# Seven block products for two row tiles in the second MLP product, other engines for some copies, and no filler products in the first batch

## The chip, the cores and the metric

The kernel runs on one core of a Trainium2 chip. The core has a matrix engine (TensorE, "PE" in the profile; its weight loads are "PEld"), three engines for elementwise work (VectorE "DVE", ScalarE "ACT", GpSimd "POOL"), SyncE ("SP"), which here only issues transfers, and 16 DMA engines. They run side by side and wait for each other by semaphores. SBUF is the working memory, PSUM holds what TensorE writes. The metric is the device time of one execution in microseconds.

## What is computed

First an attention over chunks of keys: for each query, the six best of 24 chunks of 32 keys are chosen by an upper bound on their scores, and only these (and only earlier keys) take part in the softmax. Then a layer norm and a two-layer MLP with a residual.

```python
q, k, v: (4, 8, 768, 64)                      # batch, heads, sequence, head dim
ub   = sum(max(q * k_min, q * k_max), -1)     # per chunk of 32 keys
sel  = chunk is among the top 6 of ub         # and causal
attn = softmax(where(sel & causal, q @ k.T / 8, -1e9))
x    = (attn @ v) as (4, 768, 512)
xn   = (x - mean) / sqrt(var + 1e-6) * g_ln
out  = x + relu(xn @ w_ch1) @ w_ch2           # w_ch1: 512 x 2048, w_ch2: 2048 x 512
```

## The kernel before

The work is cut into 16 pairs of heads (four to a batch; pair g belongs to batch g // 4) and, for the MLP, into eight halves (batch b, half r) of three row tiles of 128 rows each. Every piece of work is a small function, and one long string, `ORDER`, lists all calls: `smm.5.0.0` calls `smm(5, 0, 0)`, and a suffix such as `@1` sets `other[0]`, which a function may use to choose another engine. The loop at the end calls them in that order and makes every engine keep the order of its own instructions. So each engine is a queue in program order: an instruction that waits holds back all that stands behind it on its engine.

For a pair g of batches 1 to 3 (g from 4 on) the stages are:

- `ldb` loads q and k; `turn` transposes them on VectorE; `qhi`, `qlo`, `qrel` make q in two f16 parts and their positive parts; `kbound`, `kdiag` make the chunk bounds of k.
- `bounds` (L320) forms the upper bounds on TensorE, `select` chooses chunks on VectorE (L346 to L352), `maskt` and `mring` bring the mask into place.
- Operands of the scores lie in rings of four buffers, `QA`, `QB` (queries and mask rows) and `KA`, `KB` (keys). `kcopy` fills the keys on ScalarE. `qring` brings the queries into QA and QB by two transfers on SyncE's queue (L267, L268).
- `smm` (L414) makes scores into PSUM tiles `mm` (two buffers), `sexp` (L422) takes the exponential on ScalarE, `diag` (L429) masks the diagonal on GpSimd, `values` (L445) multiplies with v, `norm` (L459, L460) divides on VectorE and `pstat` takes statistics.

For a half (b, r) of the MLP: `centre` (L484, L487) makes xc = (x - mean) * g as f16 on VectorE, `rstd` (L495, L498) the reciprocal deviation, with the power on GpSimd; `xt` (L504) transposes xc by DMA; `m1` (L513) is the first product, two blocks of 128 hidden columns a call; `relu` (L525, or L523 on VectorE) writes `hT`; `m2` (L538) is the second product: a row tile has one PSUM bank `yp` and 16 products of 512 columns, four a call; `fin` (L547) adds x and stores the tile. The scale 1/deviation is applied there, after the second product:

```python
nc.vector.scalar_tensor_tensor(
    ot[:, cs], h["yp", i][:, cs], h["rstd"][:, i:i + 1], xh(b, r)[:, i].rearrange("p h d -> p (h d)")[:, cs],
    op0=ALU.mult, op1=ALU.add,
)
```

`busy(o)` (L117) multiplies constants into a part of a PSUM tile that nobody reads; `turn`, `bounds`, `smm` and others call it in batch 0, in a number that the suffix sets (none without a suffix). `w1` and `w2` load the weights in four chunks each from GpSimd's queue; chunk j of w2 holds the four blocks that `m2.b.r.i.j` uses. In PSUM the pool `ps_t` has four single banks, shared by `tr`, `ub`, `trh`, `sm` and `yp`.

Of the kernel before, what the change touches and what calls it, by code (L numbers as in the profile page):

```python
# [10 lines left out]
ALU = mybir.AluOpType  # L11
# [8 lines left out]
def kernel(  # L20
# [239 lines left out]
    def qrel(g):  # L260
        qh, ql, rh, rl = (st[g][nm][:, P:] for nm in ("qh", "ql", "rh", "rl"))
        nc.vector.tensor_scalar_max(rh, qh, 0.0)
        nc.vector.scalar_tensor_tensor(rl, qh, 0.0, ql, op0=ALU.is_gt, op1=ALU.mult)

    def qring(g, i=None):
        if i is None:
            nc.sync.dma_start(QA[g % NK][0:64, :], st[g]["qh"][0:64, :])  # L267
            nc.sync.dma_start(QB[g % NK][64:P, :], st[g]["qh"][64:P, :])  # L268
            return
        qt = st[g]["qn", i]  # L270
        a, z = span(g, i)
        nc.scalar.activation(QA[g % NK][0:64, a * P:z * P], qt[0:64, :], ACTF.Copy, scale=QS)
        nc.scalar.activation(QB[g % NK][64:P, a * P:z * P], qt[64:P, :], ACTF.Copy, scale=QS)
# [64 lines left out]
    def select(g, i=None):  # L338
# [4 lines left out]
        if g >= HP:  # L343
            ubt = smp.tile([P, NT - 1, 2, NCH], F32, name="ubt", tag="ubt", bufs=1)
            ubm = smp.tile([P, NT - 1, 2, NCH], F32, name="ubm", tag="ubm")
            nc.vector.tensor_tensor(ubt, ub[:, :, 1], causf, ALU.add)  # L346
# [131 lines left out]

    def centre(b, r):
# [3 lines left out]
        for i in range(TR):  # L483
            nc.vector.bn_aggr(h["mv"][:, i, :], h["st"][:, i])  # L484
        for i in range(TR):
            xs = xh(b, r)[:, i].rearrange("p h d -> p (h d)")
            nc.vector.scalar_tensor_tensor(  # L487
                h["xc"][:, i, :], xs, h["mv"][:, i, 0:1], gall, op0=ALU.subtract, op1=ALU.mult,
            )
# [37 lines left out]
    def last(b, r, i):  # L527
        return (b, r, i) == (B - 1, NR - 1, TR - 1)

    def m2(b, r, i, j):  # L530
# [3 lines left out]
        n, cs = 4, slice(0, DM)  # L534
        if last(b, r, i):
            n, cs = 8, slice(0, DM - P) if j < 2 else slice(DM - P, DM)
        for kt in range(n * j % KT2, n * j % KT2 + n):
            nc.tensor.matmul(  # L538
                h["yp", i][:, cs], h["hT"][:, kt, i * P:(i + 1) * P], w2b[:, kt, cs],
# [3 lines left out]
    def fin(b, r, i, e=None):  # L543
        h = hf[b, r]
        cs = (slice(0, DM), slice(0, DM - P), slice(DM - P, DM))[0 if e is None else 1 + e]
        ot = outp.tile([P, DM], F32, name="ot", tag="ot")
        nc.vector.scalar_tensor_tensor(  # L547
            ot[:, cs], h["yp", i][:, cs], h["rstd"][:, i:i + 1], xh(b, r)[:, i].rearrange("p h d -> p (h d)")[:, cs],
            op0=ALU.mult, op1=ALU.add,
        )  # L550
        s = TR * r + i
        nc.sync.dma_start(out[b, s * P:(s + 1) * P, cs], ot[:, cs])
# [4 lines left out]
        consts ld.0.0 rrows.0.0 rinit.0 ld.1.0 ld.2.0 warm.8 turn.0.qn.0 rrows.2.1@1 qpos.0.0 rrows.3.1 qring.0.0  # L557
        turn.0.kn.0 rinit.2 kbound.0.0 rinit.1 turn.1.qn.0 kcopy.0.0 ld.3.0 turn.1.kn.0 kbound.1.0 kdiag.0.0
        qring.1.0 rrows.1.0 rinit.3 turn.2.qn.0@3 ld.0.1 rrows.0.1 bounds.0.0@2 kdiag.1.0 rrows.1.1 qpos.1.0
        select.0.0 turn.2.kn.0 kcopy.2.0@1 kcopy.1.0 qpos.2.0 bounds.1.0@2 kbound.2.0 qring.2.0 maskt.0.0 select.1.0  # L560
        kdiag.2.0 turn.3.kn.0 mring.0.0@1 ld.1.1 turn.3.qn.0 kcopy.3.0 rrows.3.0 ldv.2.0 maskt.1.0 qpos.3.0
        kbound.3.0 smm.0.0.0 ldv.0.0 mring.1.0 bounds.2.0@2 select.2.0 turn.0.kn.1 qring.3.0 rrows.2.0 smm.0.0.1
        turn.1.kn.1 turn.0.qn.1 ld.2.1 kdiag.3.0 sexp.0.0.0 ldv.3.0 kcopy.0.1 qpos.0.1 kbound.1.1 sexp.0.0.1
        kbound.0.1 kcopy.1.1 ldv.1.0 kdiag.0.1 smm.1.0.0@2 bounds.3.0@2 maskt.2.0 diag.0.0 qring.0.1 bounds.0.1
        sexp.1.0.0 select.3.0 values.0.0 maskt.3.0 mring.2.0 kdiag.1.1 smm.1.0.1 select.0.1 smm.2.0.0 w1.2.3 w1.1.3
        w1.0.2 norm.0.0 sexp.1.0.1 ldb.4.qn smm.2.0.1 sexp.2.0.0 mring.3.0 maskt.0.1 ld.3.1 turn.1.qn.1 sexp.2.0.1
        qpos.1.1 ldb.5.kn mring.0.1 diag.1.0 values.1.0 norm.1.0 diag.2.0 pstat.0.0 smm.3.0.0 pstat.1.0
        turn.2.kn.1@1 sexp.3.0.0 kbound.2.1 qring.1.1 turn.4.qn smm.3.0.1@2 sexp.3.0.1 bounds.1.1 values.2.0
        smm.0.1.0 diag.3.0 select.1.1 kcopy.2.1 smm.0.1.2@1 values.3.0 sexp.0.1.0 norm.2.0 sexp.0.1.2 norm.3.0
        turn.2.qn.1 smm.0.1.1 pstat.2.0 sexp.0.1.1 kdiag.2.1@1 qpos.2.1 smm.0.1.3 qring.2.1 ldv.0.1 turn.3.kn.1  # L570
        maskt.1.1 pstat.3.0 qhi.4 kcopy.3.1 mring.1.1 diag.0.1 smm.1.1.0@2 ldb.4.kn bounds.2.1 sexp.1.1.0 sexp.0.1.3
        centre.0.0 xt.0.0.0 xt.0.0.1 select.2.1 turn.3.qn.1@3 kbound.3.1 qlo.4 smm.1.1.3 xt.0.0.2 ldb.5.qn qring.4
        maskt.2.1 turn.4.kn sexp.1.1.3 smm.1.1.2 values.0.1 kdiag.3.1 qpos.3.1 qrel.4 kbound.4 sexp.1.1.2 smm.1.1.1
        bounds.3.1 mring.2.1 sexp.1.1.1 w1.3.3 late select.3.1 kdiag.4 diag.1.1 norm.0.1 turn.5.kn m1.0.0.0 kcopy.4
        turn.5.qn relu.0.0.0 kbound.5 m1.0.0.4 ldv.1.1 qring.3.1 ldb.6.kn relu.0.0.4 w2.0.0 m1.0.0.2 relu.0.0.2
        bounds.4 pstat.0.1 m1.0.0.10 qhi.5 m1.0.0.6 relu.0.0.10 relu.0.0.6 maskt.3.1 kcopy.5@1 kdiag.5 m1.0.0.8
        m1.0.0.12 relu.0.0.8 m1.0.0.14 relu.0.0.12 ldb.6.qn smm.2.1.0 select.4 qlo.5 rstd.0.0 qrel.5 relu.0.0.14
        sexp.2.1.0 bounds.5 smm.2.1.1 smm.2.1.2 ldv.2.1 ldv.3.1 w2.1.0 turn.6.kn sexp.2.1.1 values.1.1 smm.2.1.3
        mring.3.1 diag.2.1 sexp.2.1.2 select.5 sexp.2.1.3 norm.1.1 smm.3.1.0 maskt.4 sexp.3.1.0 smm.3.1.2 kbound.6
        mring.4 maskt.5 w2.2.1 w2.3.1 sexp.3.1.2 smm.3.1.1 ldb.7.kn smm.3.1.3 sexp.3.1.1 ldb.7.qn values.2.1 qring.5  # L580
        sexp.3.1.3 mring.5 pstat.1.1 norm.2.1 smm.4.1.0 diag.3.1 sexp.4.1.0 smm.4.0.0 kdiag.6 values.3.1 m2.0.0.0.0
        norm.3.1 pstat.2.1 pstat.3.1 smm.5.0.0 kcopy.6 sexp.4.0.0 sexp.5.0.0 m2.0.0.2.0 m2.0.0.1.0 smm.4.0.1
        m2.0.0.0.1 sexp.4.0.1 turn.6.qn qhi.6 centre.0.1 qlo.6 smm.4.1.3 turn.7.kn smm.4.1.2 sexp.4.1.3 sexp.4.1.2
        m2.0.0.1.1 turn.7.qn qrel.6 smm.4.1.1 rstd.0.1 m2.0.0.2.1 kcopy.7 kbound.7 m2.0.0.0.2 m2.0.0.2.2 sexp.4.1.1
        m2.0.0.1.2 smm.5.1.0 xt.0.1.0 bounds.6 m2.0.0.2.3 select.6 xt.0.1.1 xt.0.1.2 ldb.8.kn sexp.5.1.0 qhi.7
        m1.0.1.0 qlo.7 diag.4.0 ldv.4 turn.8.kn qring.6 m1.0.1.6 relu.0.1.0 relu.0.1.6 m2.0.0.0.3 m1.0.1.14 ldb.8.qn
        kdiag.7 fin.0.0.0 qrel.7 fin.0.0.2 relu.0.1.14 ldb.9.qn diag.4.1 m1.0.1.2 kbound.8 maskt.6 ldv.5 relu.0.1.2
        ldv.6 kcopy.8 ldb.10.qn m2.0.0.1.3 qring.7 turn.8.qn mring.6 m1.0.1.4 relu.0.1.4 diag.5.0 m1.0.1.8 qhi.8
        relu.0.1.8 ldv.7 fin.0.0.1 values.4.0 norm.4.0 smm.5.0.1 bounds.7 qlo.8 smm.5.1.1 qrel.8 select.7 sexp.5.0.1
        kdiag.8 sexp.5.1.1 smm.5.1.3 values.4.1 diag.5.1 sexp.5.1.3 smm.5.1.2 ldb.9.kn values.5.0 ldb.10.kn  # L590
        ldb.12.qn sexp.5.1.2 smm.6.1.0 sexp.6.1.0 bounds.8 norm.4.1 smm.6.1.2 norm.5.0 values.5.1 sexp.6.1.2
        smm.6.1.1 sexp.6.1.1 pstat.4.1 m2.0.1.0.0 m1.0.1.10 qring.8 m1.0.1.12 m2.0.1.0.1 relu.0.1.10 relu.0.1.12
        smm.6.0.0 sexp.6.0.0 turn.9.qn maskt.7 select.8 smm.6.0.1 sexp.6.0.1 m2.0.1.0.2 pstat.4.0 maskt.8 smm.6.1.3
        qhi.9@1 diag.6.0 m2.0.1.0.3 mring.7 pstat.5.0 norm.5.1 fin.0.1.0 smm.7.0.0 diag.6.1 sexp.6.1.3 sexp.7.0.0
        smm.7.0.1 values.6.1 diag.7.0 values.6.0 mring.8 sexp.7.0.1 norm.6.1 smm.7.1.0 smm.7.1.2 values.7.0 qlo.9
        m2.0.1.2.0 norm.6.0 norm.7.0 sexp.7.1.0 smm.7.1.3 sexp.7.1.2 m2.0.1.1.0 pstat.6.0 pstat.7.0 smm.7.1.1
        ldb.11.kn sexp.7.1.3 m2.0.1.1.1 sexp.7.1.1 diag.7.1 turn.9.kn centre.1.0 xt.1.0.0 smm.8.1.0 m2.0.1.2.1
        sexp.8.1.0 smm.8.0.0 m2.0.1.2.2 kbound.9 m2.0.1.1.2 smm.8.1.2 m2.0.1.2.3 xt.1.0.2 kcopy.9 qrel.9 sexp.8.0.0
        values.7.1 sexp.8.1.2 smm.8.0.1 pstat.6.1 xt.1.0.1 smm.8.1.3 sexp.8.0.1 norm.7.1 sexp.8.1.3 kdiag.9 diag.8.1
        ldb.11.qn pstat.5.1 m2.0.1.1.3 smm.8.1.1 fin.0.1.2 bounds.9 pstat.7.1 centre.1.1 sexp.8.1.1 xt.1.1.0  # L600
        m1.1.0.0 m1.1.0.2 relu.1.0.0 xt.1.1.1 m1.1.0.4 relu.1.0.2 m1.1.0.6 relu.1.0.4 relu.1.0.6 m1.1.0.8 relu.1.0.8
# [89 lines left out]
```

## Time and profile before

| | |
|---|---|
| time, median of 3 (lowest, highest) | 288.89 us (288.71, 291.12) |
| profiled execution: device time, span of the trace | 290.76 us, 288.7 us |
| TensorE busy | 271.7 us (94%) |
| VectorE, ScalarE, GpSimd busy | 211.8, 180.8, 94.1 us |
| granted TensorE clock, mean | 0.981 |
| read from memory, written | 27.53 MB, 6.29 MB |

The span is the time from the first to the last instruction. The page divides it into 40 slices of 7.2 us, with one digit each for an engine's busy share in tenths. A group line gives a source line, engine, operation and tiles, how often, the busy time and the mean duration in ns, and then the time the engine stood idle just before. The chain of waits is followed back from the last instruction: at each step to what released it.

### The profile page before, as it was taken

Reading aid. Unit: us, or ns where it says so; the run is one execution under the profiler, and the core shown is the slowest. Engines: PE = TensorE matmul, PEld = TensorE weight load, DVE = VectorE, ACT = ScalarE, POOL = GpSimd, SP = SyncE. Lnnn points to the kernel's source line nnn. Section 1 sums busy time; section 2 is a strip of 40 time slices with the busy share of each in tenths; the row PEclk is TensorE's granted clock in tenths of the full one; section 3 lists DMA queues with packets and bytes.
Section 4 is the critical chain, followed back from the end, with each engine's and each line's share of the span. In section 5 each row is a group of like instructions: output and inputs, shape, how many; then the busy total and the mean of one; then the engine's idle time right before and its main releaser. Section 6 shows DMA issues by size and latency. Waiting matters only on the chain.

```text
span 288.7 us, 6793 instructions
## 1 busy us (share of the span) xinstructions
PE 271.7 (94%) x2628; PEld 181.8 (63%) x2628; DVE 211.8 (73%) x629; ACT 180.8 (63%) x241; POOL 94.1 (33%) x165
## 2 busy tenths in 40 slices
PE   5999999992799999999899999999999999999994
PEld 2889997671355777566656776566667745555541
DVE  5699999998079998999699979998797483221212
ACT  3688999694185977865775877667777522513210
POOL 8505615781039203182442643141072200100100
PEclk9999999998599999999999999999999999999999
DMA  6999997999949989489919691927011112310102
GB/s 141 203 179 177 202 156 126 167 151 194 139 84 70 188 162 182 78 116 133 172 29 185 112 148 20 136 81 163 16 43 59 39 20 72 93 39 36 73 0 110
DMA packets 136063, 32.42 MB, mean 112 GB/s; under 512 B 127072, under 2 KB 132960, under 8 KB 136032
## 3 DMA queue, kind: packets, MB, share of 16 engines
q1 hardware_dynamic: 106640, 24.39, 43.7%
q0 software_dynamic: 29248, 7.34, 27.4%
q8 instruction: 20, 0.33, 0.5%
q10 hardware_dynamic: 144, 0.26, 0.4%
q14 instruction: 11, 0.09, 0.1%
HBM read 27.53 MB, written 6.29 MB: 117 GB/s over the span
## 4 chain that ended last, share of the span: by engine, by line
PE 81%; DMA 8%; DVE 7%; ACT 2%; issue 1%; ACTq 0%; DVEq 0%
PE yp L538 27%; PE mm L513 25%; PE mm L414 11%; PE sm L445 6%; DMA QA<-q 3%; PE ub L333 3%; DMA xT<-xc 3%; PE ub L320 2%; ACT pt L422 2%; PE tr L236 2%; DMA raw<-in_k_dram 2%; PE tr L117 2%; DVE xc L487 1%; PE trh L361 1%; PE ub L117 1%; PE mm L117 1%
## 5 line engine op out<-in xcount | busy, mean ns | idle before, releaser
L422 ACT ACTIVATE pt<-mm 128x1024 f16<-128x1024 f32 (+2 forms) x96 | 84.6, 917 | 30.0 <-PE mm L414 28.9
L538 PE MATMUL yp<-w2b,hT 128*128 128x512 f16 (+2 forms) x400 | 94.8, 377 | 0.0
L513 PE MATMUL mm<-xT,w1b 128*128 128x384 f16 x512 | 87.9, 326 | 0.8 <-DMA xT<-xc 0.8
L525 ACT ACTIVATE hT<-mm 128x768 f16<-128x768 f32 x61 | 49.1, 810 | 59.0 <-PE mm L513 58.8
L513 PEld LDWEIGHTS <-w1b 128*128 128x128 f16 x512 | 49.5, 98 | 34.5 <-issue 0.9
L538 PEld LDWEIGHTS <-hT 128*128 128x128 f16 x400 | 38.0, 99 | 34.9 <-issue 2.1
L429 POOL TENSOR_SCALAR_AFFINE_SELECT pt<-pt 128x768 f16<-128x768 f16 x32 | 27.9, 878 | 46.6 <-ACT pt L422 46.6
L414 PE MATMUL mm<-QA,KA 128*128 128x128 f16 (+2 forms) x224 | 34.3, 248 | 8.4 <-DMA QA<-q 7.5
L547 DVE SCALAR_TENSOR_TENSOR ot<-yp,rstd,x 128x512 f32<-128x512 f32 (+2 forms) x25 | 17.9, 721 | 31.7 <-PE yp L538 18.5
L414 PE MATMUL mm<-QB,KB 128*128 128x128 f16 (+2 forms) x224 | 34.4, 248 | 0.0
L498 POOL TENSOR_TENSOR rstd<-ve,mhalf 128x3 f32<-128x3 f32 x8 | 7.0, 875 | 70.9 <-DVE ve L495 70.8
L414 PEld LDWEIGHTS <-KA 128*128 128x128 f16 x224 | 17.9, 98 | 16.5 <-DMA QA<-q 8.0
L445 PEld LDWEIGHTS <-pt 128*128 128x128 f16 x672 | 24.4, 98 | 2.3
L445 PE MATMUL sm<-va,pt 128*128 128x65 f16 x672 | 25.4, 193 | 0.0
L303 POOL TENSOR_TENSOR kc<-kc 128x24 f32<-128x24 f32 x12 | 6.2, 513 | 54.9 <-DVE kc L284 54.8
L414 PEld LDWEIGHTS <-KB 128*128 128x128 f16 x224 | 18.1, 99 | 4.4 <-issue 1.3
L475 DVE BATCH_NORM_STATS2 bst<-x 128x6 f32<-128x128 f32 x96 | 20.3, 276 | 0.0
L460 DVE TENSOR_TENSOR x<-sm,rden 128x384 f32<-128x384 f32 x32 | 17.8, 558 | 1.1
L256 DVE SCALAR_TENSOR_TENSOR q<-qnT,q 128x640 f16<-128x640 f32 x12 | 9.9, 828 | 10.1 <-ACT q L253 10.0
L487 DVE SCALAR_TENSOR_TENSOR xc<-x,mv,gall 128x512 f16<-128x512 f32 x24 | 16.7, 750 | 0.2 <-DMA xT<-xc 0.2
L206 POOL DMA_DIRECT2D va<-in_v_dram x12 | 12.8, 1064 | 0.0
L213 POOL DMA_DIRECT2D va<-in_v_dram x16 | 12.7, 795 | 0.0
(95 smaller groups left out, 347.8 us busy)
## 6 DMA issues: line engine op xcount, KB each, us to landing
out_dram<-ot SPq DMA_DIRECT2D x23, 256.0 KB, 2.3
qnb<-in_q_dram SPq DMA_DIRECT2D x48, 96.0 KB, 2.7
knb<-in_k_dram SPq DMA_DIRECT2D x48, 96.0 KB, 3.0
va<-in_v_dram POOLq DMA_DIRECT2D x12, 192.0 KB, 5.9
w1b<-in_moe_w_ch_dram POOLq DMA_DIRECT2D x4, 512.0 KB, 7.2
w2b<-in_moe_w_ch_dram POOLq DMA_DIRECT2D x4, 512.0 KB, 8.4
raw<-in_k_dram SPq DMA_DIRECT2D x16, 96.0 KB, 3.9
raw<-in_q_dram SPq DMA_DIRECT2D x16, 96.0 KB, 3.9
```

What stands on the lines that cost most here:

```text
L206: nc.gpsimd.dma_start(va[:, :, :, 0:D].rearrange("p h t d -> p (h t) d"), v[b, 2 * hp:2 * hp + 2].rearrange("h (t p) d -> p (h t) d", p=P),)
L414: nc.tensor.matmul(sc[:, hh, o:o + w * P], ks[:, t * P:(t + 1) * P], qs[:, s * P:(s + w) * P], start=True, stop=True,)
L422: nc.scalar.activation(st[g]["pt", r][:, 4 * i:4 * i + o].rearrange("p n h x -> p h n x"), st[g]["sc", r, i][:, :, 0:o * P].rearrange("p h ...
L429: nc.gpsimd.affine_select(out=dv, in_=dv, compare_op=ALU.is_ge, fill=0.0, base=0, pattern=[[0, 2 * TR], [1, P]], channel_multiplier=-1,)
L445: nc.tensor.matmul(pv[:, hh, s2, :], pt[:, where[t, s], hh, :], va[:, hh, t, 0:D + 1], start=(t == 0), stop=(t == s),)
L460: nc.vector.tensor_tensor(xh(b, r)[:, :, 2 * hp:2 * hp + 2, :].rearrange("p s h d -> p h s d"), pv[:, :, :, 0:D], rden.to_broadcast([P, 2, ...
L475: nc.vector.bn_stats(half(b, r)["st"][:, i, hp], xh(b, r)[:, i, 2 * hp:2 * hp + 2].rearrange("p h d -> p (h d)"),)
L487: nc.vector.scalar_tensor_tensor(h["xc"][:, i, :], xs, h["mv"][:, i, 0:1], gall, op0=ALU.subtract, op1=ALU.mult,)
L513: nc.tensor.matmul(hp_[:, i, 0:TR * P], w1b[:, kt, (m + i) * P:(m + i + 1) * P], h["xT"][:, kt], start=(kt == 0), stop=(kt == KT1 - 1),)
L525: nc.scalar.activation(h["hT"][:, m:m + 2], h["hp", m][:, :, 0:TR * P], ACTF.Relu, scale=HS)
L538: nc.tensor.matmul(h["yp", i][:, cs], h["hT"][:, kt, i * P:(i + 1) * P], w2b[:, kt, cs], start=(kt == 0), stop=(kt == KT2 - 1),)
L547: nc.vector.scalar_tensor_tensor(ot[:, cs], h["yp", i][:, cs], h["rstd"][:, i:i + 1], xh(b, r)[:, i].rearrange("p h d -> p (h d)")[:, cs], ...
```

## The change

**Second product.** For batches 2 and 3 the twelve row tiles are put into six pairs, and each pair is multiplied with w2 as a 2 x 2 block product by a scheme of seven block products in place of eight. The 16 hidden blocks are halved (kt 0 to 7, 8 to 15), so are the 512 output columns. `tw` makes four differences of weight blocks, once; `sc` makes four sums or differences S of the two tiles' hidden rows (128x1024 f16, VectorE); `sp` is one of the seven products, eight matmuls of 256 columns; `sx` and `so` add products from PSUM to x in place (VectorE), after which the tile is stored from x. Since rows of two tiles are mixed before the product, they must have the scale already: `centre` of these halves makes rstd first and applies it (two VectorE operations a tile in place of one).

**Other engines.** `qring` of pairs 4 and 5 copies by an engine instead of by DMA; the function's default is VectorE, and the order's suffixes (`qring.4@1`, `qring.5@2`) name ScalarE and GpSimd. `fin`, `qrel` and `select` get a form that does part of the work on ScalarE and GpSimd, used seven, six and four times.

**First batch.** No suffix asks for products on constants any more (132 before). `warm` runs 11 instead of 8 warm-up products. The whole order is written anew.

```diff
 def qrel(g):
...
-        nc.vector.tensor_scalar_max(rh, qh, 0.0)
+        if other[0]:
+            nc.scalar.activation(rh, qh, ACTF.Relu)
+        else:
+            nc.vector.tensor_scalar_max(rh, qh, 0.0)
...
 def qring(g, i=None):
+        if HP <= g < HP + 2:
+            eng = pick(nc.vector, nc.scalar, nc.gpsimd)
+            copy(eng, QA[g % NK][0:64, :], st[g]["qh"][0:64, :])
+            copy(eng, QB[g % NK][64:P, :], st[g]["qh"][64:P, :])
+            return
...
 def select(g, i=None):
-            nc.vector.tensor_tensor(ubt, ub[:, :, 1], causf, ALU.add)
+            if other[0]:
+                nc.scalar.copy(ubt, ub[:, :, 1])
+                nc.gpsimd.tensor_tensor(ubt, ubt, causf, ALU.add)
+            else:
+                nc.vector.tensor_tensor(ubt, ub[:, :, 1], causf, ALU.add)
...
+    PAIRS = (
+        ((2, 1, 0), (2, 1, 1)), ((3, 0, 0), (3, 0, 1)), ((3, 1, 0), (3, 1, 1)), ((3, 0, 2), (3, 1, 2)),
+        ((2, 0, 0), (2, 0, 1)), ((2, 0, 2), (2, 1, 2)),
+    )
 def centre(b, r):
+        if (b, r) in UNIT:
+            rstd(b, r)
...
+                nc.vector.tensor_scalar(
+                    xn, xs, h["mv"][:, i, 0:1], h["rstd"][:, i:i + 1], op0=ALU.subtract, op1=ALU.mult,
+                )
+                nc.vector.tensor_tensor(h["xc"][:, i, :], xn, gall, ALU.mult)
...
 def fin(b, r, i):
+        if other[0]:
+            nc.scalar.activation(ot, y, ACTF.Copy, scale=scale)
+            nc.gpsimd.tensor_tensor(ot, ot, xs, ALU.add)
...
+    def sc(q, k):
+        if k == 1:
+            eng.tensor_tensor(o, hpart(Bt, 0), hpart(Bt, 1), ALU.add)
+        elif k == 2:
+            eng.tensor_tensor(o, s[1], hpart(A, 0), ALU.subtract)
+        elif k == 3:
+            eng.tensor_tensor(o, hpart(A, 0), hpart(Bt, 0), ALU.subtract)
+        else:
+            eng.tensor_tensor(o, hpart(A, 1), s[2], ALU.subtract)
+    def sp(q, j):
...
+        o = s["z"][:, 0] if j in (4, 6, 7) else s["y"][:, int(j in (3, 5))]
+        lhs = {1: lambda: hpart(A, 0), 2: lambda: hpart(A, 1), 3: lambda: s[4], 4: lambda: hpart(Bt, 1),
+               5: lambda: s[1], 6: lambda: s[2], 7: lambda: s[3]}[j]()
...
+    def sx(q, j):
+        src = s["z"][:, 0] if j in (6, 7) else s["y"][:, int(j == 5)]
+        if j in (1, 6):
+            more(A, src, slice(DH, DM))
+        if j == 1:
+            more(Bt, src, slice(0, DM))
+        if j in (5, 7):
+            more(Bt, src, slice(DH, DM))
...
 ORDER
-        ... maskt.5 w2.2.1 w2.3.1 sexp.3.1.2 smm.3.1.1 ldb.7.kn smm.3.1.3 sexp.3.1.1 ldb.7.qn values.2.1 qring.5
+        ... maskt.5 smm.3.1.1 sexp.3.1.1 mring.5 qring.5@2 ldb.7.qn smm.3.1.3 sexp.3.1.3 turn.6.qn diag.3.1 values.2.1
+        norm.2.1 w2.2.1 kcopy.6 ldb.7.kn smm.4.1.0 values.3.1 pstat.2.1 rstd.0.0 m2.0.0.2.0 m2.0.0.0.0 smm.4.0.0
+        w2.3.1 pstat.1.1 sexp.4.1.0 norm.3.1 kdiag.6 pstat.3.1 smm.5.0.0 sexp.4.0.0 m2.0.0.1.0 sexp.5.0.0 m2.0.0.0.1
```

## The prediction

> **What bounds the kernel now.** I read the page first: its busy shares, and the forty slices for where TensorE is not full.
>
> ```profile
> PE 271.7 (94%) x2628; PEld 181.8 (63%) x2628; DVE 211.8 (73%) x629; ACT 180.8 (63%) x241; POOL 94.1 (33%) x165
> ...
> PE   5999999992799999999899999999999999999994
> ...
> DVE  5699999998079998999699979998797483221212
> ...
> PEclk9999999998599999999999999999999999999999
> ```
>
> TensorE (PE) is full from the second slice to the last but one, except in slices 10 and 11 (65 to 79 us), where its clock dips as well. VectorE (DVE) is nearly full in the first ten slices, busy in the middle, almost free in the last eight.
>
> Next the chain of waits, in three stretches: in the first batch, around the dip, at the end.
>
> ```profile
> 9.82 2.54 PE tr L117 x32
> 12.70 0.82 PE ub L117 x8
> ...
> 63.98 0.46 PE mm L414 x8
> ...
> 64.57 9.57 DMA QA<-q
> ...
> 74.19 1.04 PE mm L414 x8
> 75.22 3.41 PE yp L538 x8
> ...
> 277.75 6.92 PE yp L538 x32
> ...
> 284.70 0.75 DVE ot L547
> ```
>
> L117 is the product on constants, and it stands on the chain: over the first 70 us the chain gives it 6.8% + 4.7% + 4.3%, so 11.1 us. At 64.57 the ring copy of pair 5 (QA from q) is issued and lands 9.57 us later; TensorE stands for 7.49 us. Then eight 512-column products take 3.41 us, 426 ns each; at the end 32 take 6.92 us, 216 ns. I laid the order list beside the matmul starts of the trace: from 80 us on every item follows the last at its full rate, with one gap of 0.9 us at 137 us. So the later kernel is TensorE's column count.
>
> The groups give the prices that I need on the other engines.
>
> ```profile
> L547 DVE SCALAR_TENSOR_TENSOR ot<-yp,rstd,x 128x512 f32<-128x512 f32 x23 | 17.1, 742 | 25.3 <-issue 12.8 <-PE yp L538 12.1 <-POOL rstd L498 0.3
> L487 DVE SCALAR_TENSOR_TENSOR xc<-x,mv,gall 128x512 f16<-128x512 f32 x24 | 16.7, 750 | 0.2 <-DMA xT<-xc 0.2
> L498 POOL TENSOR_TENSOR rstd<-ve,mhalf 128x3 f32<-128x3 f32 x8 | 7.0, 875 | 70.9 <-DVE ve L495 70.8
> L347 DVE TENSOR_TENSOR ubm<-ub,ubt 128x240 f32<-128x240 f32 x12 | 4.9, 407 | 0.4
> ```
>
> The number before the second bar is the mean in ns.
>
> [...] the trace has two 256-column products with a weight load each in 0.22 us, so halving the columns costs no extra. [...] here the small QA copy was slow exactly while the w2 loads (8.4 us median to landing) ran.
>
> **The change, part by part.**
>
> (1) Seven products. A pair of row tiles costs 2 x 16 products of 512 columns, 32 x 0.2158 = 6.91 us. Now it costs 7 x 8 of 256, 56 x 0.1092 = 6.12. Saved 0.79, six pairs: **-4.75 us**, all on TensorE's path.
>
> (2) Ring copies of pairs 4 and 5. In the order they carry suffixes 1 and 2: pair 4 goes to ScalarE (2 x 0.82 us, as the KA casts), pair 5 to GpSimd (2 x 0.83, as its KA casts), neither to VectorE. Pair 5's starts once qh is there and nothing but diag.3.1 and a w2 issue stands behind it; it is needed about 5 us of TensorE work later. So the wait goes: -7.5 us idle, and with it the half clock: 1.04 instead of 0.45 for eight 128-column products, 3.41 instead of 1.73, and 0.5 in the next six, -2.8. Together **-10.3**.
>
> (3) Products on constants: 132 less, 11.1 us off TensorE. But from 6.5 to 64.5 us VectorE is busy 52.5 of 58 us and ScalarE 49.9, and their work up to pair 5's scores stays (VectorE) or grows by some 4 us (ScalarE: ring copy, exponentials taken earlier). VectorE's slack is mostly before 20 us (9.7 of 13.5). Between 0 and 4 us can come out; I take **-1.5**. The three additional warm-up products run while the first load is awaited (0.80 to 8.2 us): nothing.
>
> (4) What was hidden under the hole. While TensorE stood, the w2 chunks (issued at 50.1, 59.8, 61.9, 63.2) landed and xT of half (0,1) was transposed (issues 69.7 to 74.5). Now TensorE reaches w2's third chunk some 4 us after pair 5's scores, at about 69, and that chunk is issued after norm.2.1, near 64, to land 8.4 later. m1.0.1.0 is reached 9 us after those scores; centre.0.1 (2.5), three transposes (1.25 each) and a landing of 2.4 to 8.4 need 9 to 14 from its start, some 2 us after the scores. Both waits overlap: 0 to 7 us, I take **+2.5**.
>
> (5) VectorE's new work. Row sums S: 24 of 128x1024 f16, [...]. Weight differences: 4 x (0.96 + 0.42). Additions from PSUM: per pair five of 256 (0.42) and two of 512 (0.69), 3.5 us, against 1.48 for two L547. [...] In all 16.6 + 5.5 + 12 + 4.3 = 38 us more [...], in the last 110 us where VectorE is busy 82.8 of 104.9 and then 10.4 of 41.8. Some of its work leaves for ScalarE and GpSimd: 7 fin (0.74), 6 first halves of qrel (0.41), 4 ubt (0.39), 7 pairs of mask copies (0.97), together 16 us. So it fits, but at the end is tight: three pairs are 18.4 us of TensorE and 3 x (4 x 0.69 + 3.5) = 18.8 of VectorE. Products into a bank wait for the addition that reads it before; walking the last list by these prices, TensorE loses under 0.5 us, since three pairs alternate. **+0.5** [...].
>
> (6) centre of batches 2 and 3 now waits on VectorE for GpSimd's power, 0.88 us plus two handovers, four times, with the xc tiles and then xT and m1 behind it. In batch 3 the order puts 6 to 7 us of TensorE work between centre and m1, the chain needs 5.1 + 1.25 + 2.4. **+0.7** (0 to 3).
>
> (7) End: a 256-column addition (0.42) instead of 0.75 ahead of the last store, **-0.2**.
>
> fin on ScalarE and GpSimd, mask copies and K casts moved: costed at nothing, since TensorE's 250 us hide them (ScalarE 63%, GpSimd 33% busy).
>
> Sum from the profiled execution, span 288.7: -10.3 - 4.75 - 1.5 + 2.5 + 0.5 + 0.7 - 0.2 = 275.7 span. Its device time was 290.76, 2.06 over the span: **277.7 us**. The profiled run lies 1.9 over the median; I read that as a longer hole, which vanishes in both.
>
> **The rivals.** A, the above. B: another transfer takes the hole's place. For it: the DMA engines are full until 75 us and w2's last chunks are issued later than before. Against: w2's chunks have TensorE work ahead of them, the ring copy had none. If 7 of the 10.3 stay, 277.7 + 4.5 = 282.2. C: no new wait and the first batch gives its 4: 277.7 - 2.5 - 2.5 = 272.7. For it: 11 us of chain are freed; against: VectorE 98% busy from 40 to 60 us. D, the other side: the constants kept the clock up. Without them TensorE has some 27 us of work in the 38 us up to m1.0.0.0; if it falls to half clock there, 54 us, +16: 293.7, slower. For it: the dip shows what idleness does; against: the longest run of constants on the chain is 2.54 us, so the holes they leave should be well below the 7.5 us that caused the dip.
>
> **How the numbers follow.** A 0.52, B 0.20, C 0.20, D 0.08. The range runs from C (with a little below it) to above B: 272 to 283.5. Faster than 286.0 holds in A, B and C but for a heap of their upper ends: 0.88; within 1% 0.05; slower 0.07.
>
> **What would show it.** In the profile after: no QA<-q wait of PE near 65 us, no second clock dip; pair 5's copies on POOL; S sums near 0.69 us; products of 256 columns at 109 ns; what remains of PE idle between 65 and 80 us behind w2 or xT. Wrong, if the clock falls in the first 45 us, [...] or if PE idles over 5 us anywhere after 10 us.

## The result, and the profile after

| | before | after |
|---|---|---|
| time, median (lowest, highest) | 288.80 us (288.70, 291.12) | 281.44 us (280.56, 282.54) |
| ratio after / before, 95% interval | | 0.9728 (0.9663 to 0.9794) |
| profiled execution: time, span | 290.76, 288.7 us | 282.21, 280.5 us |
| TensorE, VectorE, GpSimd busy | 271.7, 211.8, 94.1 us | 260.2, 242.9, 125.3 us |

The change is faster by 7.4 us; the forecast was 11.1. The page of the changed kernel, with the same rows as were shown of the kernel before:

```profile
PE 260.2 (93%) x2627; PEld 186.3 (66%) x2627; DVE 242.9 (87%) x670; ACT 186.2 (66%) x259; POOL 125.3 (45%) x194
...
PE   6698776999999999999999999899799999999994
...
DVE  4789999589999979999789998998999799756893
...
PEclk9869997999999999999999999999999999999999
```

Before, slices 10 and 11 stood at 2 and 7 out of ten; now they are full. In exchange TensorE is thinner in slices 4 to 7 (21 to 49 us), with low digits of the clock in slices 2, 3 and 7, and in slices 26 and 29 (175 to 182 and 196 to 203 us), where it was full. VectorE is at 7 to 9 tenths up to slice 35 (245 us), except in slices 1 and 8; before, it had 1 to 3 tenths from slice 34 on.

The waits of TensorE in the first 80 us (engine and line, what it waited for; total, times, longest in us):

```profile
PE mm L544 <- DMA xT<-xc: 2.4, 1, 2.4
...
PE tr L236 <- issue: 1.7, 1, 1.7
```

The first is ahead of m1.0.0.0 at 45.4 us, the second at 10.5 us. Between 66 and 80 us there is no wait. The groups of the new work, with the mean ns after the second bar's comma:

```profile
L625 DVE TENSOR_TENSOR S<-hT 128x1024 f16<-128x1024 f16 x6 | 4.1, 685 | 0.6 <-ACT hT L556 0.6
...
L655 DVE TENSOR_TENSOR x<-yb,x 128x256 f32<-128x256 f32 x18 | 7.5, 419 | 2.3 <-PE yb L646 2.0
...
L516 DVE TENSOR_TENSOR xc<-xn,gall 128x512 f16<-128x512 f32 x12 | 9.4, 785 | 0.4
...
L513 DVE TENSOR_SCALAR xn<-x,mv,rstd 128x512 f32<-128x512 f32 x12 | 7.9, 659 | 4.2 <-POOL rstd L529 3.9
```

The row sums take 685 ns and the narrow additions 419, close to the 0.69 and 0.42 us of the forecast, which were the author's estimates: no row of before shows them. By the starts of the matmuls eight 256-column products take 0.873 us, 109 ns each. But VectorE idles 3.9 us for GpSimd's power (L529), in four waits of about 1 us. Two of them, ending at 171.6 and 191.7 us, lie in the stretch where TensorE waits for VectorE. The chain of waits between 176 and 200 us is almost VectorE alone (start, duration, what):

```profile
176.75 0.82 DVE q L256
...
187.16 1.22 DVE q L256
188.38 0.86 DVE kc L291
189.25 0.86 DVE kc L292
190.11 0.43 DVE mv L505 x3
190.80 0.90 POOL rstd L529
191.72 1.10 DVE xn L513
192.85 1.24 DVE xc L516
...
196.69 1.30 DVE r L266
198.35 0.96 DVE m L363 x10
```

By the starts of its matmuls, TensorE loses 5.2 us between 157 and 200 us (before: nothing), in nine waits; the last two, 1.8 us together, lie between 197.5 us and the maskt at 199.9 us. (The view of waits counts only idle time with modelled ends, and gives about 3.5.) The operand `r` of the bounds and the selection (L363) stand behind centre.2.1 on VectorE, and centre.2.1 holds it from 190.0 to 196.7 us.

**Three landmarks**, as starts of the same call in both traces: the scores of pair 5 (smm.5.0.0) 74.2 before, 69.9 after; m1.1.0.0 126.5 and 118.9; m1.2.0.0 186.5 and 179.9. TensorE's last product ends at 284.7 and 276.9. So 6.6 us are won by m1.2.0.0, and only 1.1 us behind it (98.2 against 97.1 us), although all the new products lie there. (One call of `bounds`, about 0.7 us of TensorE, stood behind this landmark before and now stands ahead of it.)

One thing is needed to read the times below: on the three chips of the experiments the kernel before took 279.3 to 293.7 us, and in 5 of its 33 executions (279.3 to 282.3 us, recorded mean clock 0.997 to 1.000; all others 284.7 and more, 0.975 to 0.993) the loss seems to have been absent, though none of these five was traced, and beside them alone neither the ring copies nor the whole change shows a gain.

### The profile page after: what moved, and what is told of

It is laid out like the page before. It is cut to its first block, busy times and chain, and to the rows that moved or that the text cites. A ratio compares the mean times of both kernels' runs of the same rounds, so it can differ in the third digit from the quotient of the medians.

```text
span 280.5 us, 6899 instructions
## 1 busy us (share of the span) xinstructions
PE 260.2 (93%) x2627; PEld 186.3 (66%) x2627; DVE 242.9 (87%) x670; ACT 186.2 (66%) x259; POOL 125.3 (45%) x194
## 4 chain that ended last, share of the span: by engine, by line
PE 68%; DVE 14%; ACT 5%; issue 5%; DMA 4%; POOL 2%; SPq 1%; DVEq 0%; POOLq 0%
PE mm L544 24%; PE yp L563 12%; PE mm L426 9%; PE ya L646 7%; PE yb L646 6%; PE sm L457 5%; ACT pt L434 2%; PE ub L341 2%; DVE bst L487 2%; DMA xT<-xc 2%; PE tr L236 2%; PE ub L328 1%; DMA raw<-in_q_dram 1%; DVE kc L292 1%; DVE q L256 1%
## 5 line engine op out<-in xcount | busy, mean ns | idle before, releaser
L544 PE MATMUL mm<-xT,w1b 128*128 128x384 f16 x512 | 89.1, 330 | 3.5 <-DMA xT<-xc 2.4
L556 ACT ACTIVATE hT<-mm 128x768 f16<-128x768 f32 x58 | 46.5, 811 | 43.8 <-PE mm L544 38.4
L441 POOL TENSOR_SCALAR_AFFINE_SELECT pt<-pt 128x768 f16<-128x768 f16 x32 | 31.8, 1000 | 37.9 <-ACT pt L434 37.7
L563 PE MATMUL yp<-w2b,hT 128*128 128x512 f16 x192 | 47.8, 379 | 0.4 <-DVE x L472 0.3
L563 PEld LDWEIGHTS <-hT 128*128 128x128 f16 x192 | 17.9, 98 | 15.7 <-issue 0.8
L529 POOL TENSOR_TENSOR rstd<-ve,mhalf 128x3 f32<-128x3 f32 x8 | 7.0, 876 | 33.1 <-DVE ve L526 33.1
L646 PEld LDWEIGHTS <-S 128*128 128x128 f16 x192 | 18.7, 98 | 2.8
L646 PEld LDWEIGHTS <-hT 128*128 128x128 f16 x144 | 14.0, 98 | 1.9
L655 DVE TENSOR_TENSOR x<-ya,x 128x256 f32<-128x256 f32 (+1 forms) x24 | 12.7, 552 | 2.7 <-PE ya L646 2.5
L581 POOL TENSOR_TENSOR ot<-ot,x 128x512 f32<-128x512 f32 x7 | 9.5, 1361 | 9.8 <-ACT ot L580 9.6
L256 DVE SCALAR_TENSOR_TENSOR q<-qnT,q 128x640 f16<-128x640 f32 x12 | 11.8, 987 | 1.2 <-ACT q L253 1.1
L206 POOL DMA_DIRECT2D va<-in_v_dram x12 | 12.8, 1069 | 0.2
```

Of the source, the lines that this page charges most:

```text
L206: nc.gpsimd.dma_start(va[:, :, :, 0:D].rearrange("p h t d -> p (h t) d"), v[b, 2 * hp:2 * hp + 2].rearrange("h (t p) d -> p (h t) d", p=P),)
L256: nc.vector.scalar_tensor_tensor(st[g]["ql"][:, P:], st[g]["qn", None][:, P:], QS, st[g]["qh"][:, P:], op0=ALU.mult, op1=ALU.subtract,)
L441: nc.gpsimd.affine_select(out=dv, in_=dv, compare_op=ALU.is_ge, fill=0.0, base=0, pattern=[[0, 2 * TR], [1, P]], channel_multiplier=-1,)
L544: nc.tensor.matmul(hp_[:, i, 0:TR * P], w1b[:, kt, (m + i) * P:(m + i + 1) * P], h["xT"][:, kt], start=(kt == 0), stop=(kt == KT1 - 1),)
L556: nc.scalar.activation(h["hT"][:, m:m + 2], h["hp", m][:, :, 0:TR * P], ACTF.Relu, scale=HS)
L563: nc.tensor.matmul(h["yp", i], h["hT"][:, kt, i * P:(i + 1) * P], w2b[:, kt, :], start=(kt == 0), stop=(kt == KT2 - 1),)
```

## Experiments

Theory H: the whole gain is the hole at 66 us; the ring copies alone would give it, and what the seven products save is given back elsewhere. Rival P: the gain comes from the products, and the rest cancels. To be told apart besides: why the hole is there (slow transfers, or the order of SyncE's queue), and where the 4.75 us are given back (the first batch without constants, the new centre, the sums). The times are medians of all executions of a run, lowest and highest in brackets. Chips differ, so each stands beside the kernel before on its chip: 287.87 on the first, 289.94 on the second, 288.79 on the third. For the waits a yardstick by stretch is better than the total: from the start of m1.2.0.0 to the end of TensorE's last product, called the **last stretch** here, which should depend little on what happened before; it is compared mainly within the new order. In two profiles of the changed kernel it is 97.1 and 98.5 us, the second with half clock from 195.0 to 198.5 us, so a difference of 1.5 us is not yet one.

### First chip: one part of the change at a time

**The kernel before with the ring copies alone.** `qring` as in the change, pair 4 on ScalarE, pair 5 on GpSimd:

```diff
     def qring(g, i=None):
+        if HP <= g < HP + 2:
+            eng = pick(nc.vector, nc.scalar, nc.gpsimd)
+            copy(eng, QA[g % NK][0:64, :], st[g]["qh"][0:64, :])
+            copy(eng, QB[g % NK][64:P, :], st[g]["qh"][64:P, :])
+            return
 ORDER
-        qring.4 ... qring.5
+        qring.4@1 ... qring.5@2
```

> The kernel before with the ring copies alone: pair 4's on ScalarE, pair 5's on GpSimd, nothing else. Theory 'hole' (step 2 of the prediction): the 7.5 us wait of TensorE near 67 us and the half clock behind it go, 288.8 - 10.3 + 1.9 (the profiled run was 1.9 over the median) = about 280, 279 to 282. Rival 'another transfer takes its place' (B): w2 or xT is waited for instead, at least 5 of the 10 us stay, 284 or more.

Measured 281.06 us (280.06 to 282.12), 6.8 under before. Its page:

```profile
PE   6899998998999999999999999999999999999994
PEclk9999999999999999999999999999999999999999
```

No hole, no dip, and smm.5.0.0 at 68.1 us. Two copies of 1.6 us on engines with room do as much as the whole change; it is also about what the kernel before takes in its two lowest executions on this chip (279.29 and 281.26).

**The changed kernel with the ring by transfers again.**

```diff
-        if HP <= g < HP + 2:
+        if False:
 ORDER
-        qring.4@1 ... qring.5@2
+        qring.4 ... qring.5
```

> The changed kernel with the ring copies of pairs 4 and 5 by transfer again. Theory 'hole': pair 5's scores wait for the transfer as in the kernel before, 5 to 10 us more than 281.4, so 286 to 291. Rival: in the new order the w2 chunks are issued later and pair 5's copy has the transfers to itself, so the wait is under 3 us and the time under 284.

Measured 281.12 us (280.25 to 285.60): the hole did not come back in the profiled execution, nor in the median. The new order issues pair 5's transfer at 53.5 us, before the loads of pair 7; it takes 7.1 us to land, and is needed at about 66. So the change has removed the hole twice over, by the engine and by the order.

**The constants put back into the changed kernel** (132, at the 11 calls that had them):

```diff
 ORDER
-        turn.2.qn.0 bounds.0.0 bounds.1.0 bounds.2.0 smm.1.0.0 bounds.3.0 ...
+        turn.2.qn.0@3 bounds.0.0@2 bounds.1.0@2 bounds.2.0@2 smm.1.0.0@2 bounds.3.0@2 ...
```

> The changed kernel with the products on constants of the first batch put back at the eleven calls that had them before (same suffixes, so 132 products, about 11 us of TensorE). Theory 'clock': in the changed kernel the half clock from 11.4 to 18.3 us and from 45.6 to 49.0 us is the price of the idle TensorE; with the constants back the first dip vanishes, m1.0.0.0 starts no later than now (45.4 us) and the time falls by 1 to 4 us, to 277.5 to 280.5. Rival 'queues': the first batch is set by VectorE, ScalarE and the loads; the dips lie in slack, and the time stays at 281.4 or rises by up to 5 us for the 11 us of products.

Measured 284.17 us (279.57 to 288.18), not faster in the median, though two of its six executions (279.57 and 280.24) are within the expected window. In its profile the half clock at 11 to 18 us is gone. A later one is there, from 43.6 to 50.5 us, since TensorE again stood for the transposed half:

```profile
PE mm L544 <- DMA xT<-xc: 3.3, 1, 3.3
```

So in this execution filling TensorE's idle time at 11 to 18 us did not bring the first batch back: the wait for xT is a loss of its own, which constants don't fill.

**Eight products in the changed kernel's order.** The calls tw, sc and sx go, each sp is a quarter of an ordinary second product (or two of them), so becomes fin:

```diff
 ORDER
-        sc.4.1 ... sp.4.1 ... sx.4.1 ... sp.4.6 ... so.4.0
+        m2.2.0.0.0 ... m2.2.0.0.1 ... fin.2.0.0
```

> The changed kernel with the ordinary second product in batches 2 and 3: each of the seven block products of a pair is replaced, at its place in the order, by one or two of the eight ordinary groups of four 512-column products; the sums S, the weight differences and the additions to x are left out and each tile is finished by one addition. TensorE gets 4.75 us more, VectorE about 29 us less. Theory 'TensorE alone counts': time rises by 4.75, 286.2. Theory 'VectorE bounds 176 to 200 us': the waits of TensorE there (5.5 us in all) belong to the additional work on VectorE, of which the sums are a part; then time rises by less than 3 us, to under 284.5. If the waits at 179 to 200 us stay as they are (over 4 us) though the sums are gone, they come from the rest of VectorE's queue there.

Measured 289.26 us (284.36 to 290.97), more than either expectation. The total of the profiled execution holds a bad first batch (xT waited for 4.5 us, half clock four times before 51 us), so the stretch is read: the last stretch is 101.9 us against 97.1 in the changed kernel (97.0 and 97.3 in the two runs above). The difference, 4.8, is the forecast saving of 4.75. TensorE's waits stay: they now lie between 157 and 202 us and come to 6.3 us against 5.2, so they don't come from the sums.

### Second chip: why the hole, and what took the saving

**The kernel before with one call moved.** The ring of pair 5 stays a transfer; it is only issued ahead of the loads of pair 7:

```diff
 ORDER
-        smm.3.1.1 ldb.7.kn smm.3.1.3 sexp.3.1.1 ldb.7.qn values.2.1 qring.5
+        smm.3.1.1 qring.5 ldb.7.kn smm.3.1.3 sexp.3.1.1 ldb.7.qn values.2.1
```

> The kernel before with one token moved: the transfers of pair 5's ring copy stand ahead of the load of pair 7 (ldb.7.kn, ldb.7.qn) in SyncE's queue instead of behind it; they remain transfers. Theory 'queue': in the kernel before the copy is issued only at 64.6 us because the loads ahead of it wait for a free load buffer; issued some 6 us earlier or more, even a transfer of 7 to 10 us lands in time, the hole goes, and the time is 279 to 282 as with the copies on ScalarE and GpSimd. Rival 'slow transfer': the small copy is slow beside the w2 loads whenever it is issued, and half of the hole or more stays: 284 or more.

Measured 283.07 us (280.17 to 284.25), 6.9 under before and 1.1 over the expected window, at a recorded mean clock of 0.991 to 1.000. SyncE's timeline (start, duration, what), first of the kernel before:

```profile
59.85 4.60 SPq L194 DMA_DIRECT2D qnb<-in_q_dram  x4
64.57 3.00 SPq L267 DMA_DIRECT2D QA<-q  x1
67.67 1.24 SPq L268 DMA_DIRECT2D QB<-q  x1
```

and of this kernel:

```profile
53.59 3.76 SPq L267 DMA_DIRECT2D QA<-q  x1
57.46 0.71 SPq L268 DMA_DIRECT2D QB<-q  x1
58.21 3.65 SPq L194 DMA_DIRECT2D knb<-in_k_dram  x4
61.97 9.44 SPq L194 DMA_DIRECT2D qnb<-in_q_dram  x4
```

In the first, QA stands behind four load pieces that take 4.6 us to issue; in the second those pieces take 9.4 us, and nothing that TensorE needs soon stands behind them. QA takes 6.3 us to land here against 9.6, but above all it starts 11 us earlier. So the hole is what a queue in program order does with an urgent small transfer behind loads that need not go yet. That QA is slow at that time (9.6 us, where the median of the twelve QA transfers of the kernel before is 2.5) makes it long; the order makes it a hole.

**The ring copies alone, without the constants** (the first kernel of these experiments, the eleven suffixes taken off):

```diff
 ORDER
-        turn.2.qn.0@3 bounds.0.0@2 bounds.1.0@2 ...
+        turn.2.qn.0 bounds.0.0 bounds.1.0 ...
```

> The kernel before with the ring copies of pairs 4 and 5 on ScalarE and GpSimd (281.06 with that alone) and without the 132 products on constants of the first batch. Theory 'clock': TensorE falls to half clock at least once before 46 us, and the 11 us of products taken off come to nothing or less: 280 to 285. Rival 'chain': the constants lay on the chain, and at least 3 us come out: under 278.

Measured 283.94 us (281.32 to 286.07), against 283.07 for the kernel with one call moved: 0.9 more, with overlapping ranges. Taken off alone the constants are worth nothing that these runs can tell. In the profiled execution (285.71) m1.0.0.0 started at 50.3 us instead of 44.5, and the short fp32 products of the bounds (L338) ran slow. Their busy time by stretch, here and with the constants (stretch, its length, TensorE busy, weight loads busy, clock, DMA share, GB/s):

```profile
20.00:35.00 15.00, 6.36 (x30) 6.20 (x30) 1.00 1.13 180
```

```profile
20.00:35.00 15.00, 4.01 (x32) 3.81 (x32) 1.00 1.25 187
```

212 ns against 125 for one, while the clock column says 1.00 in both. From start to start it is so for every shape: here 128-column f16 products follow each other at 107 ns and the fp32 ones at 213, up to 34 us, and from there on at 56 and 112 as in the other kernel. 107 and 213 are also the steps in the half clock that is on record in the changed kernel from 11.4 to 18.2 us. So this execution ran at half clock up to 34 us, and the clock record does not have it. m1.0.0.0 came 5.8 us later; other waits differ between the two executions as well.

**The power earlier.** Statistics and rstd leave centre and go where the last statistics of the half are done:

```diff
-    def centre(b, r):
+    def stat(b, r):
         h = hf[b, r]
...
         if (b, r) in UNIT:
             rstd(b, r)
+
+    def centre(b, r):
+        h = hf[b, r]
+        if "mv" not in h:
+            stat(b, r)
...
 ORDER
-        pstat.11.0 ... pstat.11.1 ... pstat.15.1 ... pstat.15.0
+        pstat.11.0 stat.2.0 ... pstat.11.1 stat.2.1 ... pstat.15.1 stat.3.1 ... pstat.15.0 stat.3.0
```

> The changed kernel, with the statistics of the four halves of batches 2 and 3 (aggregation, variance and GpSimd's power) taken out of centre and put right behind the last pstat of each half, so that VectorE has other work while GpSimd makes the power. Theory 'VectorE bounds 176 to 200 us, the wait for rstd is part of it': the waits of 1.0 us ahead of xn go, TensorE's waits between 157 and 200 us (5.5 us) fall by 1 to 2 us and the time to about 280. Rival 'slack': the wait is hidden by other waits, no change against 281.4.

Measured 282.99 us (281.15 to 285.69), the last stretch 97.5 us, no better than 97.1, and TensorE's waits there are again 5.2 us. The wait for the power went and another took its place:

```profile
DVE xn L518 <- DMA out_dram<-ot: 2.4, 1, 2.4
DVE xn L518 <- POOL rstd L534: 0.3, 1, 0.3
```

xn shares its two buffers with the tile `ot` that fin stores, so now VectorE waits for a store. The wait was moved, not removed, and this run doesn't decide about the power.

**Eight products and the old centre**, the scale applied at the end as before:

```diff
-    UNIT = {t[:2] for pair in PAIRS for t in pair}
+    UNIT = set()
```

The order calls `rstd` of these four halves by itself again, ahead of their `fin`.

> As the run with eight products in the changed order, and also with the old form of centre: one VectorE operation a tile, no wait for the power, the scale applied at the end as before. Theory 'centre': the waits of TensorE between 157 and 200 us that stayed with eight products (6.4 us there) fall by 2 us or more, because centre's second operation and its wait for the power were what VectorE lacked time for. Rival 'GpSimd': they stay within 1 us of that, and come from VectorE operations lengthened by GpSimd's larger share and from the new order itself.

Measured 282.97 us (281.29 to 287.83). TensorE's waits between 157 and 202 us fall to 2.9 us from 6.3, and the last stretch to 98.9 us from 101.9 with the new centre. So the new form of centre costs 3.0 us of TensorE's time there. The kernel before needs 98.2 us for this stretch. That closes the account of it: 4.8 us saved by the seven products, 3.0 given back by centre, 0.7 by the new order and the work moved to other engines (1.4 with the call of `bounds` that now stands ahead), which no run takes apart.

### Third chip: can both losses be taken away?

**The changed kernel again**, as the measure for the three after it.

> The changed kernel once more, beside the three runs below on one chip, as their measure. Chips differed by 1 to 2 us so far. Expected 280.5 to 284; in the profile a wait of 1 to 6 us for xT ahead of the first m1.0.0.0 near 45 us with half clock beside it, and 4 to 6 us of TensorE waits between 157 and 200 us. If the waits in the first batch are a matter of chance in the transfers, one of these two is missing or the size differs from 2.4 us.

Measured 282.92 us (279.32 to 285.99). This profiled execution (279.32) has no wait for xT, m1.0.0.0 starts at 42.0 us instead of 45.4 and smm.5.0.0 at 65.1 instead of 69.9, although half clock at 14 to 17 us is there again. The transposes landed in 2.3 to 2.6 us; in the first profile in 2.3 to 4.4. The losses of the batch 2 stretch are there (4.7 us of waits, and they end in half clock from 195.0 to 198.5 us, which the first profile did not have), and the last stretch is 98.5 us. On this chip the change is 5.9 us under before in the median, but not under the two lowest executions of before (281.65 and 282.26).

**A load of w1 moved out of the transposes' way.**

```diff
 ORDER
-        bounds.3.1 w1.3.3 m1.0.0.0 sexp.1.1.1 kcopy.4 kbound.4 turn.5.kn kdiag.4 select.3.1 m1.0.0.4
+        bounds.3.1 m1.0.0.0 sexp.1.1.1 kcopy.4 kbound.4 turn.5.kn kdiag.4 select.3.1 m1.0.0.4 w1.3.3
```

> The changed kernel with the last load of w1's third chunk (0.5 MB, issued near 41 us, just beside the transposes of the first half) put behind m1.0.0.4. Theory T (the transposes of xc into xT are slow because that load takes the transfer engines): the wait for xT ahead of m1.0.0.0 falls under 1 us, no half clock at 44 to 51 us, 2 to 3 us less than the changed kernel beside it. Theory V (the first batch is late because VectorE's work is late, and the transposes start late for that reason): the wait changes by less than 1 us and the time by less than 1 us. Rival: the load is needed soon after, and TensorE waits for w1 near 50 us instead: same or slower.

Measured 281.03 us (279.51 to 282.71). Its profile has no wait for xT, and one of 0.6 us for w1, at 52.1 us, a small one of the kind that the rival named. But the changed kernel just above had no wait for xT either, so the profile decides nothing. The medians differ by 1.9 us with spreads of 6.7 and 3.2 us, and the lowest executions (279.32 and 279.51) do not differ, so no gain is shown.

**centre as before, then the scale in place.** One fp32 operation a tile as in the kernel before, and then one f16 operation that multiplies by rstd, so that the power is computed beside the first three:

```diff
-            if (b, r) in UNIT:
-                if i == 0:
-                    xn = outp.tile([P, DM], F32, name="xn", tag="ot")
-                nc.vector.tensor_scalar(
-                    xn, xs, h["mv"][:, i, 0:1], h["rstd"][:, i:i + 1], op0=ALU.subtract, op1=ALU.mult,
-                )
-                nc.vector.tensor_tensor(h["xc"][:, i, :], xn, gall, ALU.mult)
-                continue
             nc.vector.scalar_tensor_tensor(
                 h["xc"][:, i, :], xs, h["mv"][:, i, 0:1], gall, op0=ALU.subtract, op1=ALU.mult,
             )
+        if (b, r) in UNIT:
+            for i in range(TR):
+                nc.vector.tensor_scalar_mul(h["xc"][:, i, :], h["xc"][:, i, :], h["rstd"][:, i:i + 1])
```

> The changed kernel with centre of batches 2 and 3 as before (one operation a tile, no wait for GpSimd's power), and then one f16 operation a tile in place that multiplies by rstd, so that the power is computed beside the first three. Theory R (the wait for rstd and the two fp32 operations are what the new centre costs): the waits of TensorE between 157 and 200 us fall from 5 to 6 us to about 3, as with the old centre, and the time by 2 to 3 us. Theory N (that stretch is bound by the sum of VectorE's work, whatever the form): the waits move and their sum falls by less than 1 us; time the same within 1 us.

Measured 278.03 us (275.81 to 282.95), 4.9 under the changed kernel on this chip (more than the 2 to 3 expected, with ranges that overlap), 10.8 under before and 3.6 under even the lowest execution of before on this chip. VectorE's timeline around centre.2.1 (start, duration, what; in brackets the idle time before it and what ended it), first of the changed kernel, then of this one:

```profile
190.55 0.17 DVE L526 TENSOR_SCALAR ve<-mv 128x3 f32<-128x3 f32 x1
191.72 1.09 DVE L513 TENSOR_SCALAR xn<-x,mv,rstd 128x512 f32<-128x512 f32 x1 [1.00 <-POOL rstd L529]
192.85 1.23 DVE L516 TENSOR_TENSOR xc<-xn,gall 128x512 f16<-128x512 f32 x1
...
196.69 1.30 DVE L266 SCALAR_TENSOR_TENSOR r<-q 128x640 f16<-128x640 f16 x1
```

```profile
187.09 0.17 DVE L521 TENSOR_SCALAR ve<-mv 128x3 f32<-128x3 f32 x1
187.21 2.08 DVE L510 SCALAR_TENSOR_TENSOR xc<-x,mv,gall 128x512 f16<-128x512 f32 x3
189.21 2.09 DVE L515 TENSOR_SCALAR xc<-xc,rstd 128x512 f16<-128x512 f16 x3
191.22 0.81 DVE L266 SCALAR_TENSOR_TENSOR r<-q 128x640 f16<-128x640 f16 x1
```

From ve to r it was 6.1 us and is now 4.1, and nothing waits for the power. TensorE's waits between 157 and 200 us fall to 2.5 us, and the last stretch to 94.1 us. That is 3.0 less than in the first profile of the changed kernel, as much as the old centre gave with eight products, and 4.4 less than in the one on this chip, with its half clock. (The f16 operation's median is 348 ns; the 2.09 us for three lie beside 2.19 us of GpSimd's L441.)

The same profile shows a wait that the changed kernel did not have, ahead of m1.0.1.0 at 77.7 us:

```profile
PE mm L539 <- DMA xT<-xc: 2.2, 1, 2.2
```

TensorE was ready there earlier than in the first profile of the changed kernel, where m1.0.1.0 started at 78.9 us. But in the profile of the changed kernel on this chip it started at 74.6 us, earlier still, and had waited for 0.1 us only.

**Both edits, and 48 constants in three early calls.**

```diff
 ORDER
-        turn.2.qn.0 ... bounds.0.0 ... bounds.1.0
+        turn.2.qn.0@3 ... bounds.0.0@2 ... bounds.1.0@2
```

> Both of the above, and in addition the products on constants of the first three calls (turn of pair 2, bounds of pairs 0 and 1, issued by 20 us, 2 to 3 calls' worth of the 132). If T and R hold and half clock at 11 to 18 us comes from the idle time that the constants filled: no half clock after 11 us, and 276 to 279 us, below both kernels. If V and N hold: within 1 us of the changed kernel.

Measured 279.25 us (278.69 to 279.84), just over the expected window and not below the kernel with the scale in place; half clock came later instead, at 22 to 29 and 39 to 42.6 us. The last stretch is again 94.1 us. What differs is the spread: 1.2 us, against 7.1 for the scale in place alone and 6.7 for the changed kernel. Both versions are faster in the median than the kernel before and the changed one (the longest execution of this one, 279.84, is close to the shortest of the changed kernel, 279.32); neither is shown to be better than the other.

## Why the prediction was right, and where its sizes were off

The time lies in the range and on the forecast side. Theory H fits the runs: the ring copies alone give about as much as the whole change, and of the 4.8 us of the seven products 3.0 are given back by the new centre and 0.7 by the rest of the new order. By the prediction's steps, in the span of the profiled execution (forecast 275.7 us, measured 280.5):

- **(1) Seven products, -4.75.** Right: 109 ns a product of 256 columns (from start to start the kernel before has 215.8 ns at 512 columns and 109.0 at 256), and 4.8 us between eight and seven products in the same order.
- **(2) Ring copies, -10.3.** Right in effect: no wait, no dip, pair 5's copies on GpSimd. With the ring copies alone the span falls from 288.7 to 279.2 us, 9.5 of the 10.3. In the medians it is 6.8, and 6.9 with one call moved, probably because the hole differs from one execution of the kernel before to the next and the profiled one had a long one, as the prediction supposed; only that one was traced. The reason given, a transfer slow beside the w2 loads (9.6 us to landing; 6.3 when issued 11 us earlier), was half of it; the queue order is what can be acted on.
- **(3) Constants, -1.5.** Mis-sized. smm.5.0.0 was reached at 69.9 us; before, TensorE stood ready for it at 66.7. With 0.9 us for four products of 512 columns that the new order puts ahead of it, the first batch lost 2.3 us instead of gaining 1.5. But in another execution of the same kernel it was reached at 65.1, so the term is not one number. Of eight profiles of the new order without constants, four reached smm.5.0.0 at 65.1 to 66.1 us and four at 69.9 to 72.2; of these four, three waited 2.4 to 6.0 us for xT ahead of m1.0.0.0, and the fourth ran at half clock for 10 us up to 50.5 us. Taking the constants off alone moved the time by 0.9 us, which isn't resolved.
- **(4) What the hole hid, +2.5.** 0 in the profiled execution, where TensorE came late, through (3). Of the four profiles that reached smm.5.0.0 at 65.1 to 66.1 us, one (scale in place) waited 2.2 us for xT ahead of m1.0.1.0, the other three 0 to 0.5 us. So the wait can occur, but coming early does not suffice for it, and 2.5 was too much.
- **(5) VectorE's sums, +0.5.** Right for the sums: 685 ns, and no wait of TensorE in the last 20 us. The other new prices were estimates of the author too: 0.69 for the wide additions (measured 0.68), 0.96 and 0.42 for the two sizes of weight differences (0.95 to 1.38 and 0.41 to 1.08). VectorE's total was not right: it is busy 31.1 us more, where the prediction's terms give 22 (38 more, 16 less).
- **(6) The new centre, +0.7.** The term most mis-sized with a clear cause: 3.0 us, the end of its stated range of 0 to 3. Its two operations took 659 and 785 ns in the mean (545 and 692 at the lowest), where the one of the kernel before took 750; over twelve tiles that is 8.3 us more, and the 4.3 of the prediction were an estimate that no trace shows. The prediction costed the wait for the power by the chain from centre to m1, and VectorE's 38 us more work by the whole of the last 110 us. It did not ask which other work stands behind centre on VectorE between 176 and 200 us, where VectorE works almost without a gap (busy 22.6 of 24 us) and TensorE waits for its operands. There VectorE's time, and not the wait alone, shows in TensorE's.
- **(7)** The tail from TensorE's last product to the end is 3.6 us, before 4.1, so -0.5 where -0.2 was forecast.

The sum of what was off: (3) +3.8, (4) -2.5, (5) -0.5, (6) with all waits of that stretch +4.5 (5.2 against 0.7), (7) -0.3, together 5.0, of the 4.8 us by which the span was longer. That the total came within 4 us is in part luck: (3) and (4) missed in opposite directions. One of the prediction's own signs of being wrong came true, for the clock fell at 11.4 us, and yet the time stayed in the range. So Rival D (half clock in the first batch) was right in kind and wrong in size: it happens in most profiles, in spells of 3.4 to 17 us. Where it lasted up to 34 us, in the kernel without constants, m1.0.0.0 came 5.8 us later and not the 16 forecast for 38 us. Rival B (another transfer takes the hole's place) names what the xT wait does, at 45 us rather than 65 to 80; its 282.2 us happens to be nearest.

Left open: whether moving the w1 load or the 48 constants narrows the spread, as they were only run together with the scale in place (the load once alone); what the 2.5 to 2.9 us of waits are that TensorE keeps in the batch 2 stretch with either cheaper centre; and why the first batch ends in a wait or in half clock in some executions and not in others, beyond the landing times of the transposes.

## What to carry to other kernels

Before replacing a transfer by an engine's work, look at what stands ahead of it in its issuing queue: moving one call gave as much as the copies, and as much as the whole change. When a change lowers the bottleneck engine's work, cost the new work on the others in the stretch where they are full, not against their slack over the whole; here a step on VectorE with no idle time around it took 3.0 of 4.75 us. And compare stretches between two landmarks, not totals, where the total moves by several us from one execution to the next; the stretch moves too, here by 1.5 us.

## What the runs showed of the hardware

**VectorE took longer in some places beside GpSimd's work.** The same instruction shape varies like this in the changed kernel (lowest, median, highest ns):

```profile
L516 DVE TENSOR_TENSOR xc<-xn,gall x12: 692/693/1228, 172.7 to 243.2; 128x512 f16<-128x512 f32 x12
```

and in the timeline the long one at 192.85 us and the 1.30 us of r at 196.69 lie beside these on GpSimd:

```profile
191.67 1.87 POOL L441 TENSOR_SCALAR_AFFINE_SELECT pt<-pt 128x768 f16<-128x768 f16 x2
...
196.19 1.13 POOL L356 TENSOR_TENSOR ubt<-ubt,causf 128x240 f32<-128x240 f32 x1
```

Of the 24 executions of L513 and L516, the fifteen that no instruction on GpSimd overlaps took 545 to 547 ns (L513) and 692 to 693 (L516). Of the nine that one overlaps, two (L513) took 546 ns all the same, and seven took 874 to 1094 (L513) and 720 to 1228 (L516). From 219 to 277 us, where GpSimd is busy for 1.7 us, every L516 takes 0.69 us. GpSimd's own small operations are longer near 195 us as well: L318 took 0.61 us at 194.93 us against 0.26 at 182.91. The product that makes q (L256 in both kernels) rose from 828 to 987 ns in the mean, as GpSimd's busy time rose from 94 to 125 us; its three longest executions (1143, 1298 and 1819 ns) all overlap instructions on GpSimd. So moving work to GpSimd probably took back part of what it freed; the traces show that the two coincide, not why. The prediction had no term for it.

**Half clock after short waits.** In the changed kernel the clock fell at 11.4 us, within a wait of 1.7 us among short products, and stayed down for 6.8 us. In its second profile it fell at 195.0 us too (mean 0.96 from 157 to 200 us), in a stretch where TensorE's waits come to 4.7 us; in the first profile they come to 5.2 us there, and the clock stayed at 1.00. In the hole of the kernel before it fell 2.6 us after TensorE stopped (69.3 and 66.7 us). So in these runs no one length of a wait tells whether the clock falls: 1.7 us was enough once.
